# Three PSUM banks in turn for layer 2 and one for layer 1, in place of two and two

## The chip, the cores and the metric

The kernel runs on one core of a Trainium2 chip, alone. The metric is the device time of one execution in microseconds; the time of a kernel is the median of its runs.

## The reference

The input `x` has 2 x 4096 tokens of 192 numbers. Three things are done to it, and only the first looks at more than one token:

```python
out = np.einsum('hk,bskhg->bshg', softmax(weight), x_unf)   # causal, 7 taps, 8 heads of 24
h = x @ w_in;  g = h * np.clip(h + 3, 0, 6) / 6;  x = g @ w_out      # layer 1, 192 -> 2048 -> 192
h = x @ w_in
P = a[0] + a[1]*h + a[2]*h**2 + a[3]*h**3
Q = 1 + abs(b[0])*abs(h) + abs(b[1])*h**2
x = (P / (Q + 1e-6)) @ w_out                                          # layer 2, the same sizes
```

All of it is float32. The kernel makes each float32 product of sums of products of a high and a low part, so that one layer's tile takes several matmuls.

## The kernel before, in words

The 8192 tokens are cut into 16 blocks of 512; the last block is cut in two once more, so there are 17 units (0 to 14 whole, 15 and 16 of 256 tokens). The 2048 hidden numbers are cut into 16 parts of 128. One tile is 128 hidden numbers of a unit, 128 x 512 elements; a unit of half width takes two parts at once, so that its tiles have that shape as well. Each layer has 15 x 16 + 2 x 8 = 256 tiles, and the planner's time runs in steps of one tile of layer 2.

A tile of layer 1: five matmuls `mm1` (L501) put h into a PSUM bank; ACT makes `u` from it (L545), DVE makes `g` from `u` and the bank (L550), and with that the bank is free; ACT rounds the high part (`hi1`, L557), POOL takes the low part (`lo1`, L563), and five matmuls (`mm2` and `mm2l`, L515 to L520) add it to the unit's two sums in other banks. After 16 tiles the sums become the input of layer 2.

A tile of layer 2: five matmuls `mm3` (L501) put h into a bank; ACT makes `A` = |h| (L615) and `T` (`t1`, L627), DVE two steps of the numerator (`t2` L642, `t3` L654, both read the bank), ACT or POOL and then POOL make the denominator `S` (L634, L636, L648), ACT its reciprocal root (`R`, L659), whose square (`RR`, L663) is written into the bank, DVE a Newton step (`w` L668), the numerator's last step, into the bank (`p2` L672), and the product `G` (L677), and with that the bank is free. Then `hi2` on ACT (L683), `lo2` on POOL (L692), and five matmuls `mm4` and `mm4l`.

PSUM has eight banks. Four hold the sums of the two layers. The other four are `bank0` to `bank3` (L218): layer 1 takes 0 and 1 in turn (`site1`, L522; in the beginning unit 0 has bank 0 and unit 1 bank 1), layer 2 takes 2 and 3 in turn (`site2`, L528; in the last unit, two tiles in four take 0 and 1). A third kind of work needs a bank for a short time: the convolution (`conv`, L442, on xn), the transposes of its result (`flip`, L457) and of the output (`out_tr`, L708 and L709). `transient` (L769) gives them the bank that layer 1 does not use at that moment, `1 - [...]` of the list `line1`. While the weights are being split into high and low parts, in the first 19 steps, banks 2 and 3 also serve as scratch for that (`weights`, L727).

In SBUF, T, S, A, g2h and g2l of layer 2 have two buffers each (pool `p2`), u, g1h and g1l of layer 1 two each (`p1`). The weights come in through four buffers `raw` of 128 x 1024 (pool `sg`) and five `m` of 128 x 512 (`sgm`), which have little to do later.

The order on every engine is fixed ahead by the class `Issue`. Each operation is entered with `at` (L83) under an engine, a duration, what it reads and writes, and a sort key: its step plus an offset from `OFF` (`OFF0` in the beginning, `OFFT` in the last unit). `graph` (L87) derives the dependences, also those from a ring of buffers or a bank that comes round, and `order` (L125) lists the operations engine by engine: of those that are ready it takes the one with the smallest key plus a bias of its kind, within a look-ahead (`AHEAD`, `LOOK`). The engines run these lists strictly in order. Layer 1 runs ahead: its units 0 and 1 go together in steps 0 to 16 (`when1`, L756), then one unit per 17 steps; layer 2 begins in step 19 (`LAG`) with one unit per 16 steps (`when2`, L763). Layer 1 is done some 12 steps before layer 2.

Of the kernel before, what the change touches and what calls it, by code (L numbers as in the profile page):

```python
# [7 lines left out]
F32 = mybir.dt.float32  # L8
F32R = mybir.dt.float32r
# [5 lines left out]
D1 = 2  # L15
# [2 lines left out]
PER = 17  # L18
PERH = 13
CONV = -11  # L20
CONV2 = 1.4221
PAT = [1, 2]
PAT0 = [1, 2]
PATT = [1, 2]
W1P = [-2.7212, -2.1926]
W2P = [2.853, 2.0712]
WARM = 12
LOENG = [0, 1, 0, 1]
CLAMP = [0, 1, 0, 1]
WPART = dict(c0=0.0035, v0=-0.1744, vs=0.2224, h0=0.4972, hs=0.0194, l0=0.7095, ls=0.0191)  # L30
HEAD = 19.51
TAIL = -8.47
AHEAD0 = dict(P=23.739, A=33.318, V=6.679, G=43.933, S=999.0)
LOOK0 = dict(P=22, A=218, V=3, G=275, S=0)
AHEADT = dict(P=10.587, A=26.994, V=26.868, G=6.693, S=999.0)
LOOKT = dict(P=716, A=250, V=265, G=983, S=0)
OFF0 = dict(
    mm2=-1.6078, mm2l=-1.3327, x2mh=-0.6482, x2mg=-0.8371, lo1=1.3047, x2ml=-0.5563, x2al=-1.1236, x2mc=-0.2459,
    mm1=-0.2559, hi1=0.8615, g=0.1758, u=0.1648, x2ah=-1.1817,
)  # L40
OFFT = dict(
    sq=0.2665, mm4l=-0.2221, x2al=3.1822, RR=1.6307, q2=1.4163, oa=-0.1248, lo2=4.0164, mm3=-0.5662, q1=1.0926,
    A=-0.4555, t3=0.9018, w=2.2795, G=3.1778, x2mh=1.9241, x2mg=2.1784, x2ml=2.9393, hi2=3.9844, R=1.562,
    p2=2.2993, tr=0.9036, q=1.6358, os=1.3787, mm4=-0.289, x2mc=3.187,
)
D10 = 3
D2T = 5
X0 = -5.1761
X1 = -0.8706
XW = [-103.8655, -103.0862, -56.7048, -45.6279]  # L50
BIAS = dict(l1=1.269, dec=1.5585, conv=1.482, out=-3.4178, x2=0.5443)
AHEAD = dict(P=10.034, A=30.747, V=25.077, G=8.984, S=999.0)
LOOK = dict(P=11, A=158, V=144, G=308, S=0)
OFF = dict(
    sq=-0.1906, q1=-0.0053, q2=0.0282, mm3=-0.5496, mm1=1.0929, mm4=0.0716, tr=1.357, mm2=1.3942, A=-0.5102,
    t1=0.082, u=1.2441, R=0.2631, RR=0.3824, hi2=1.3091, hi1=2.1384, S=-0.339, lo2=1.8031, lo1=2.9099,
    q=-3.3161, t2=0.2092, t3=0.3818, w=0.5827, p2=0.9559, G=1.047, g=1.2615, cv=1.6807, x1ah=1.6042,
    x1al=1.9194, x1bh=1.5836, x1bl=1.795, x2ah=2.2232, x2al=3.1818, x2mh=1.7614, x2mg=2.9447, x2mc=2.2852,
    x2ml=1.8296, oa=0.8152, oc=0.9804, os=1.5101, mm2l=1.6382, mm4l=0.4334,
)  # L60


class Issue:
# [10 lines left out]
        mm1=1133, mm3=1133, conv=774, flip=445, out_tr=533, u=477, hi1=520, hi2=520, t1=568, R=520, RR=520,  # L74
# [106 lines left out]
def conv_moe_moe_kernel(ctx: ExitStack, tc: tile.TileContext, x, weight, w_in1, w_out1, w_in2, w_out2,  # L181
# [8 lines left out]
    B, S, DM = x.shape  # L190
# [5 lines left out]
    C = 512  # L196
# [4 lines left out]
    NU = len(units)  # L201
    steps = [NF * n // C for _, _, n in units]
# [4 lines left out]
    p1 = ctx.enter_context(tc.tile_pool(name="p1", bufs=2))  # L207
    p2 = ctx.enter_context(tc.tile_pool(name="p2", bufs=2))
# [4 lines left out]
    sgm = ctx.enter_context(tc.tile_pool(name="sgm", bufs=5))  # L213
# [4 lines left out]
    bank = [ps.tile([128, C], F32, name=f"bank{k}") for k in range(4)]  # L218
# [95 lines left out]
    raw = {}  # L314
# [207 lines left out]
    def site1(b, i):  # L522

        if b == 1:
            return p2, ("T", "g2h", "g2l"), 1
        return p1, ("u", "g1h", "g1l"), i % 2 if b else 0

    def site2(b, i):  # L528

        if b == NU - 1 and i % 4 >= 2:  # L530
            return p1, ("raw", "raw", "m", "g1h", "g1l"), i % 2
        return p2, ("S", "T", "A", "g2h", "g2l"), 2 + i % 2

    class L1:
        @staticmethod
# [57 lines left out]
    class L2:  # L593
# [5 lines left out]

        @staticmethod  # L600
        def mm3(b, i):
            h2[b, i] = bank[site2(b, i)[2]]
            product_in(1, b, i, [x2[b, k] for k in ("x2ah", "x2al", "x2m1", "x2ml")], h2[b, i])

        @staticmethod
        def A(b, i):
            v2[b, i] = d = {}
            p, tags, _ = site2(b, i)
            if tags[0] == "raw":
                st = sg.tile([128, 2 * C], F32, tag="raw", name="ST")  # L610
# [12 lines left out]

        @staticmethod
# [102 lines left out]
    def weights(t_load, t, kind, l, c, turn):  # L727
# [40 lines left out]

    def transient(t, mm, ns, *args, r, kind):  # L769

        if t > end1 or mm in (conv, flip) and args[0] == 1:
            k = fill[0] = fill[0] + 1
            tag = f"acc{int(t < end1)}{k % 2}"
            key = (tag, ("free", k))
            at(t, "P", ns, mm, lambda: pa.tile([128, C], F32, tag=tag, name="fb"), *args, r=r, w=[key], kind=kind)
        else:
            k = fill[0] % 2 if t < 0 else 0 if t < steps[0] else 1 - [k for w, k in line1 if w <= t][-1]
            fill[0] += 1
            key = (f"bank{k}", ("free", fill[0]))
            at(t, "P", ns, mm, lambda: bank[k], *args, r=r, w=[key], kind=kind)  # L780
        return key

    fill = [0]
    taken = {when1(b, 0) + CONV + k for b in range(2, NB) for k in range(4)}
    for b in range(NU):
        bl, _, cols_u = units[b]
        for i in range(steps[b]):
            n, t, c = (b, i), when1(b, i), i * C // cols_u // 2
            _, (U, Hi, Lo), k = site1(b, i)
            U, Hi, Lo, k = (U, (1, n)), (Hi, (1, n)), (Lo, (1, n)), (f"bank{k}", (1, n))  # L790
# [14 lines left out]
            _, (S_, T, A, Hi, Lo), k = site2(b, i)
            if S_ == "raw":
                S_, T = ("raw", n), ("rawT", n)
            else:
                S_, T = (S_, n), (T, (2, n))
            A, Hi, Lo, k = (A, n), (Hi, (2, n)), (Lo, (2, n)), (f"bank{k}", (2, n))  # L810
# [36 lines left out]
        t = when2(b, steps[b] - 1) + (D2T if b == NU - 1 else D2)  # L847
# [3 lines left out]
        for hf in range(cols_u // 256):  # L851
            t = int(t + 1.9)
# [10 lines left out]
        t = when1(b, 0) + CONV if not first else X1 if b else X0  # L863
# [98 lines left out]
```

## Time and profile before

| | us |
|---|---|
| median of 3 runs | 1310.19 (1309.35 to 1311.1) |
| the profiled execution | 1310.59 |
| its span, first to last instruction | 1308.8 |

The span is 1.79 us shorter than the time of the same execution. Busy time of an engine is the time in which at least one of its instructions runs; matmuls overlap, and their ends are modelled, so that PE counts as busy also where the next matmul starts a little late. PEld is the weight load that precedes each matmul. Idle time of an engine that isn't the bottleneck costs nothing.

### The profile page before, as it was taken

The page shows a single profiled execution, that of the slowest core. Times are in us where ns is not written, and L with a number is a line of the kernel's source. Part 1 is how long each engine was busy: PE and PEld are TensorE (multiplying, and loading weights), DVE is VectorE, ACT ScalarE, POOL GpSimd, SP SyncE. Part 2 cuts the span into 40 slices and gives each one's busy share as a digit, 9 for nine tenths or more (in the row PEclk, how much of TensorE's full clock was granted, in tenths as well). Part 3 has the DMA queues.
Part 4 walks back from the last instruction along what each step waited for, and adds up shares of the span by engine and source line. Part 5 has one row for each costly group of instructions (what it writes and reads, how often), then busy time and mean ns, then how long its engine had stood idle before and what let it go on. Part 6 is the DMA issues. An engine that isn't in the chain of part 4 may idle for free.

```text
span 1308.8 us, 18723 instructions
## 1 busy us (share of the span) xinstructions
PE 1277.1 (98%) x6072; PEld 1039.8 (79%) x6072; DVE 1164.5 (89%) x1808; ACT 1192.1 (91%) x2183; POOL 1123.6 (86%) x954
## 2 busy tenths in 40 slices
PE   8999999999999999999999999999999999999977
PEld 5776877878788888888888888888787888888866
DVE  6999898988988889889898898988989889898897
ACT  5788999999999999999999999999999999999996
POOL 4998898888898888988889888888988898888976
PEclk9999999999999999999999999999999999999998
DMA  6440000000000000000000000000000000000000
GB/s 176 139 151 18 16 1 13 16 7 22 1 14 14 13 16 7 22 1 13 16 13 16 13 1 17 13 16 13 1 28 0 2 13 1 13 2 13 1 13 13
DMA packets 29002, 28.62 MB, mean 22 GB/s; under 512 B 2156, under 2 KB 25832, under 8 KB 28904
## 3 DMA queue, kind: packets, MB, share of 16 engines
q1 hardware_dynamic: 28744, 27.27, 7.0%
q8 instruction: 47, 0.77, 0.2%
q14 instruction: 51, 0.42, 0.1%
q10 hardware_dynamic: 160, 0.16, 0.0%
HBM read 21.13 MB, written 6.30 MB: 21 GB/s over the span
## 4 chain that ended last, share of the span: by engine, by line
PE 64%; DVE 16%; ACT 15%; issue 3%; POOL 2%; DMA 1%; SPq 0%; DVEq 0%; ACTq 0%; POOLq 0%
PE bank L501 30%; PE acc L518 6%; PE acc L515 6%; PE acc L520 6%; PE acc L519 6%; PE acc L516 6%; ACT bank L663 2%; DVE bank L672 2%; DVE S L668 2%; DVE T L654 2%; DVE T L677 2%; ACT A L659 2%; PE bank L442 2%; DVE T L642 2%; ACT A L615 2%
## 5 line engine op out<-in xcount | busy, mean ns | idle before, releaser
L648 POOL TENSOR_TENSOR S<-A,S 128x512 f32<-128x512 f32 x252 | 327.0, 1298 | 73.9 <-ACT S L634 56.2
L692 POOL TENSOR_TENSOR g2l<-T,g2h 128x512 fp32r<-128x512 f32 x252 | 327.7, 1301 | 47.7 <-ACT g2h L683 45.0
L563 POOL TENSOR_TENSOR g1l<-u,g1h 128x512 fp32r<-128x512 f32 x240 | 311.8, 1300 | 6.5 <-ACT g1h L557 4.6
L668 DVE SCALAR_TENSOR_TENSOR S<-S,bank 128x512 f32<-128x512 f32 x252 | 172.6, 685 | 80.6 <-ACT bank L663 75.1
L501 PE MATMUL bank<-low,B 128*128 128x512 f32 (+1 forms) x544 | 205.4, 378 | 0.0
L654 DVE SCALAR_TENSOR_TENSOR T<-T,coef,bank 128x512 f32<-128x512 f32 x252 | 188.3, 747 | 8.3
L672 DVE SCALAR_TENSOR_TENSOR bank<-T,coef,bank 128x512 f32<-128x512 f32 x252 | 188.9, 749 | 0.4
L642 DVE SCALAR_TENSOR_TENSOR T<-T,coef,bank 128x512 f32<-128x512 f32 x252 | 186.8, 741 | 2.0 <-ACT T L627 1.7
L550 DVE SCALAR_TENSOR_TENSOR u<-u,bank 128x512 f32<-128x512 f32 x240 | 163.1, 681 | 18.6 <-ACT u L545 18.1
L677 DVE SCALAR_TENSOR_TENSOR T<-S,bank 128x512 f32<-128x512 f32 x252 | 172.8, 686 | 7.2
L683 ACT ACTIVATE g2h<-T 128x512 fp32r<-128x512 f32 x252 | 159.3, 632 | 20.9 <-DVE T L677 17.8
L663 ACT ACTIVATE bank<-A 128x512 f32<-128x512 f32 x256 | 153.2, 598 | 24.4 <-DVE T L654 20.2
L627 ACT ACTIVATE T<-bank,coef 128x512 f32<-128x512 f32 x252 | 173.5, 688 | 1.8 <-POOL g2l L692 1.7
L659 ACT ACTIVATE A<-S 128x512 f32<-128x512 f32 x252 | 157.8, 626 | 13.2 <-POOL S L648 12.2
L557 ACT ACTIVATE g1h<-u 128x512 fp32r<-128x512 f32 x240 | 151.4, 632 | 10.2 <-DVE u L550 9.9
L545 ACT ACTIVATE u<-bank 128x512 f32<-128x512 f32 x240 | 141.6, 592 | 4.2 <-PE bank L501 2.9
L501 PE MATMUL bank<-x2ah,Ah 128*128 128x512 f32 (+1 forms) x272 | 110.3, 406 | 12.5 <-DVE T L677 9.9
L636 POOL TENSOR_SCALAR S<-A,coef 128x512 f32<-128x512 f32 x126 | 98.1, 779 | 24.1 <-ACT A L615 23.1
L501 PEld LDWEIGHTS bank<-low,B 128*128 128x128 f32 x544 | 102.4, 188 | 19.6
L515 PE MATMUL acc<-g2l,O 128*128 128x512 f32 (+1 forms) x280 | 111.5, 400 | 1.7 <-POOL g2l L692 1.4
L518 PE MATMUL acc<-g2h,O 128*128 128x512 f32 (+1 forms) x280 | 108.4, 387 | 1.5 <-ACT g2h L557 0.7
L501 PE MATMUL bank<-x1ah,Ah 128*128 128x512 f32 (+1 forms) x272 | 105.1, 386 | 3.2 <-DVE u L550 2.9
(135 smaller groups left out, 3216.6 us busy)
## 6 DMA issues: line engine op xcount, KB each, us to landing
raw<-in_moe_w_out_dram SPq DMA_DIRECT2D x16, 384.0 KB, 3.7
out_dram<-osb SPq DMA_DIRECT2D x32, 192.0 KB, 2.0
xn<-in_x_dram SPq DMA_DIRECT2D x14, 384.0 KB, 3.4
raw<-in_moe_w_in_dram SPq DMA_DIRECT2D x16, 256.0 KB, 2.9
raw<-in_moe_w_in_dram SPq DMA_DIRECT2D x16, 128.0 KB, 3.4
xn<-in_x_dram SPq DMA_DIRECT2D x16, 96.0 KB, 3.2
xn<-in_x_dram SPq DMA_DIRECT2D x2, 288.0 KB, 6.3
band<-line_d SPq DMA_DIRECT2D x2, 256.0 KB, 3.9
```

What stands on the lines that cost most here:

```text
L501: nc.tensor.matmul(out=dst[:, cs], lhsT=w[nm][:, fs], rhs=m, start=(k == 0), stop=(k == 4))
L515: nc.tensor.matmul(out=a, lhsT=o[:, 0:128], rhs=g, start=False, stop=sp)
L518: nc.tensor.matmul(out=a, lhsT=o[:, 0:128], rhs=g, start=st, stop=False)
L563: nc.gpsimd.tensor_tensor(out=gl, in0=v1.pop((b, i)), in1=f32(g1[b, i][0]), op=ALU.subtract)
L642: stt(out=d["T"], in0=d["T"], scalar=coef[:, 2:3], in1=h2[b, i], op0=ALU.add, op1=ALU.mult)
L648: (nc.gpsimd if k else nc.vector).tensor_tensor(out=d["S"], in0=d["A"], in1=d["S"], op=ALU.add if k == 1 else ALU.mult)
L654: stt(out=d["T"], in0=d["T"], scalar=coef[:, 1:2], in1=h2[b, i], op0=ALU.add, op1=ALU.mult)
L659: act(out=d["A"], in_=d["S"], func=ACTF.Abs_reciprocal_sqrt, bias=c1)
L668: stt(out=d["S"], in0=d["S"], scalar=c1, in1=h2[b, i], op0=ALU.add, op1=ALU.mult)
L672: stt(out=h2[b, i], in0=v2[b, i]["T"], scalar=coef[:, 0:1], in1=h2[b, i], op0=ALU.add, op1=ALU.mult)
L677: stt(out=d["T"], in0=d["S"], scalar=2.0, in1=h2.pop((b, i)), op0=ALU.subtract, op1=ALU.mult)
L692: e.tensor_tensor(out=gl, in0=v2.pop((b, i))["T"], in1=f32(gh), op=ALU.subtract)
```

## The change

Layer 1 has only bank 0 (and unit 1, as before, bank 1). Layer 2 takes banks 3, 1, 2 in turn, and in the last unit every fourth tile takes bank 0. The buffers go with the bank: tiles on banks 2 and 3 use the pool `p2` as before, a tile on bank 1 has S and T in a `raw` buffer and A, g2h and g2l in `m` buffers, a tile on bank 0 has S and T in two `u`, A in an `m`, and `g1h` and `g1l`. So T, for one, has three places in place of two. A transient takes the bank of the next tile of layer 2 that begins more than 1.2 steps after it (`NEXT`). All sort keys and most biases and look-aheads get other values; the operations, their engines, forms and number stay the same, and so do `LAG`, `PER`, `PERH`, D1 and D2.

```diff
-        return p1, ("u", "g1h", "g1l"), i % 2 if b else 0
+        return p1, ("u", "g1h", "g1l"), 0
+
+    def spare2(b, i):
+        return b == NU - 1 and i % 4 == 3
+
+    turn2 = {}
+    for u in range(NU):
+        for i in range(steps[u]):
+            turn2[u, i] = 0 if spare2(u, i) else 1 + (2 + sum(v > 0 for v in turn2.values())) % 3
 
     def site2(b, i):
-        if b == NU - 1 and i % 4 >= 2:
-            return p1, ("raw", "raw", "m", "g1h", "g1l"), i % 2
-        return p2, ("S", "T", "A", "g2h", "g2l"), 2 + i % 2
+        k = turn2[b, i]
+        return (("u", "u", "m", "g1h", "g1l"), ("raw", "raw", "m", "m", "m"))[k] if k < 2 else ("S", "T", "A", "g2h", "g2l"), k
+
+    def place2(b, i, j):
+        tag = site2(b, i)[0][j]
+        p = dict(u=p1, g1h=p1, g1l=p1, m=sgm).get(tag, p2)
+        t = p.tile([128, C], F32R if tag[0] == "g" else F32, tag=tag, name=tag)
+        return t.bitcast(F32R) if tag == "m" and j > 2 else t
...
-    line1 = [(when1(u, i), i % 2) for u in range(NU) if u != 1 for i in range(steps[u])]
+    line2 = [(when2(u, i), turn2[u, i]) for u in range(NU) for i in range(steps[u])]
...
-            k = fill[0] % 2 if t < 0 else 0 if t < steps[0] else 1 - [k for w, k in line1 if w <= t][-1]
+            k = fill[0] % 2 if t < 0 else 0 if t < steps[0] else [k for w, k in line2 if w + NEXT > t][0]
```

Of the keys in `OFF`, those that the prediction speaks of (in steps; before, after): mm1 1.0929, 0.3745; u 1.2441, 0.6259; g 1.2615, 0.8453; mm3 -0.5496, -0.4599; t1 0.082, 0.1215; G 1.047, 1.3429; lo2 1.8031, 2.5013; tr (a transient's matmuls) 1.357, 1.7345; cv (the convolution's copy out) 1.6807, 2.4719.

## Rows read from the trace of the kernel before

**Rows 1.** the page's first part: busy us (share of the span) xinstructions of each engine

```profile
PE 1277.1 (98%) x6072; PEld 1039.8 (79%) x6072; DVE 1164.5 (89%) x1808; ACT 1192.1 (91%) x2183; POOL 1123.6 (86%) x954
```

**Rows 2.** stretches: from:to us, length, engine busy us (xcount), PE clock, DMA share, GB/s

```profile
20.60:112.70 92.10, 85.60 (x375) 64.70 (x373) 86.44 (x176) 73.89 (x156) 79.75 (x76) 1.00 0.44 131
112.70:1244.00 1131.30, 1125.36 (x5311) 921.40 (x5311) 1012.31 (x1516) 1061.28 (x1926) 993.92 (x827) 1.00 0.04 11
1244.00:1300.80 56.80, 44.86 (x303) 40.41 (x304) 52.82 (x81) 48.15 (x87) 43.64 (x38) 0.93 0.04 11
1300.80:1308.80 8.00, 3.81 (x23) 3.45 (x22) 1.12 (x2) 1.51 (x3) 0.01 (x1) 0.71 0.08 26
```

**Rows 3.** the same view, a stretch of eight whole units of layer 2

```profile
410.80:1013.60 602.80, 602.43 (x2770) 491.19 (x2769) 539.51 (x807) 567.02 (x1028) 530.05 (x441) 1.00 0.04 12
```

**Rows 4.** groups by line on PE in that stretch; xcount, busy us, mean ns, idle before

```profile
L442 PE MATMUL bank<-xn,band 128*122 128x120 f32 x112 | 14.4, 272 | 0.1
L709 PE MATMUL bank<-perm,oac 128*128 128x64 f32 x64 | 9.9, 248 | 0.0
L457 PE MATMUL bank<-perm,x1n 122*128 122x122 f32 (+1 forms) x70 | 9.6, 267 | 0.0
```

**Rows 5.** that stretch, line 677 alone (once per tile of layer 2)

```profile
410.80:1013.60 602.80, 87.77 (x128) 1.00 0.04 12
```

**Rows 6.** that stretch, line 550 alone (once per tile of layer 1)

```profile
410.80:1013.60 602.80, 81.58 (x120) 1.00 0.04 12
```

**Rows 7.** timeline, PE: start us, duration us, engine, line, operation [idle before <-releaser]

```profile
700.75 0.39 PE L501 MATMUL bank<-x1ah,Ah 128*128 128x512 f32 x1
...
701.88 0.39 PE L501 MATMUL bank<-x2ah,Ah 128*128 128x512 f32 x1
...
706.55 0.39 PE L501 MATMUL bank<-x2ah,Ah 128*128 128x512 f32 x1
...
707.69 0.39 PE L501 MATMUL bank<-x1ah,Ah 128*128 128x512 f32 x1
...
710.41 1.01 PE L442 MATMUL bank<-xn,band 128*122 128x120 f32 x8
...
711.18 0.48 PE L501 MATMUL bank<-x2ah,Ah 128*128 128x512 f32 x1
```

**Rows 8.** timeline, ACT and DVE, the same stretch

```profile
708.38 0.59 ACT L545 ACTIVATE u<-bank 128x512 f32<-128x512 f32 x1
...
709.12 0.68 DVE L550 SCALAR_TENSOR_TENSOR u<-u,bank 128x512 f32<-128x512 f32 x1
...
709.43 0.61 ACT L545 ACTIVATE u<-bank 128x512 f32<-128x512 f32 x1
...
709.72 0.68 DVE L677 SCALAR_TENSOR_TENSOR T<-S,bank 128x512 f32<-128x512 f32 x1
...
711.46 0.57 ACT L450 ACTIVATE x1n<-bank 122x480 f32<-122x480 f32 x1 [0.38 <-PE bank L442]
...
711.76 0.68 DVE L550 SCALAR_TENSOR_TENSOR u<-u,bank 128x512 f32<-128x512 f32 x1
```

**Rows 9.** waits from 130 to 1177 us: who waited for whom: us, times, longest us

```profile
DVE S L668 <- ACT bank L663: 67.7, 138, 1.4
...
PEld bank L501 <- DVE T L677: 15.7, 51, 1.0
...
PEld bank L442 <- DVE u L550: 2.5, 8, 0.6
...
PEld bank L708 <- DVE u L550: 1.7, 5, 0.5
...
PEld bank L501 <- DVE u L550: 1.3, 3, 0.6
```

**Rows 10.** waits from 1225 us to the end

```profile
PEld bank L501 <- DVE T L677: 10.0, 9, 2.1
```

More of the change, by code (lines that the diff above doesn't have):

```diff
@@ L20 @@
 CONV = -11
-CONV2 = 1.4221
+CONV2 = 1.5208
 PAT = [1, 2]
@@ L24 @@
 PATT = [1, 2]
-W1P = [-2.7212, -2.1926]
-W2P = [2.853, 2.0712]
+W1P = [-2.511, -1.6167]
+W2P = [3.1007, 2.6842]
 WARM = 12
@@ L29 @@
 CLAMP = [0, 1, 0, 1]
-WPART = dict(c0=0.0035, v0=-0.1744, vs=0.2224, h0=0.4972, hs=0.0194, l0=0.7095, ls=0.0191)
+WPART = dict(c0=0.0894, v0=0.1498, vs=0.1355, h0=1.0583, hs=0.051, l0=1.1051, ls=0.1176)
 HEAD = 19.51
 TAIL = -8.47
[L33 to L36, printed above, removed]
+AHEAD0 = dict(P=29.159, A=34.598, V=14.704, G=33.913, S=999.0)
@@ L37 @@
+LOOK0 = dict(P=181, A=111, V=0, G=135, S=0)
+AHEADT = dict(P=2.417, A=11.5, V=26.627, G=8.091, S=999.0)
+LOOKT = dict(P=52, A=118, V=110, G=1311, S=0)
 OFF0 = dict(
-    mm2=-1.6078, mm2l=-1.3327, x2mh=-0.6482, x2mg=-0.8371, lo1=1.3047, x2ml=-0.5563, x2al=-1.1236, x2mc=-0.2459,
-    mm1=-0.2559, hi1=0.8615, g=0.1758, u=0.1648, x2ah=-1.1817,
+    mm2=-1.5338, mm2l=-1.3337, x2mh=-0.4568, x2mg=0.4102, lo1=1.1872, x2ml=-0.3679, x2al=0.2982, x2mc=0.2088,
+    mm1=-1.0623, hi1=0.8438, g=-0.5149, u=-0.6917, x2ah=-0.9173,
@@ L40 @@
 )
 OFFT = dict(
-    sq=0.2665, mm4l=-0.2221, x2al=3.1822, RR=1.6307, q2=1.4163, oa=-0.1248, lo2=4.0164, mm3=-0.5662, q1=1.0926,
-    A=-0.4555, t3=0.9018, w=2.2795, G=3.1778, x2mh=1.9241, x2mg=2.1784, x2ml=2.9393, hi2=3.9844, R=1.562,
-    p2=2.2993, tr=0.9036, q=1.6358, os=1.3787, mm4=-0.289, x2mc=3.187,
+    sq=-0.3575, mm4l=-1.2305, x2al=3.5317, RR=2.1537, q2=1.3964, oa=-1.0444, lo2=3.4316, mm3=-0.3947, q1=1.2682,
+    A=-0.3856, t3=1.0523, w=2.4254, G=2.4661, x2mh=1.7969, x2mg=2.2183, x2ml=2.2136, hi2=3.3057, R=2.0466,
@@ L45 @@
+    p2=2.4646, tr=1.3163, q=1.0405, os=5.7408, mm4=-1.4005, x2mc=3.3094,
 )
 D10 = 3
+NEXT = -1.2
 D2T = 5
[L48 to L53, printed above, removed]
-OFF = dict(
[L55 to L59, printed above, removed]
+X0 = -4.2712
@@ new lines @@
+X1 = -0.9752
+XW = [-101.8602, -99.0414, -56.2823, -44.9956]
+BIAS = dict(l1=0.2014, dec=0.3628, conv=0.3916, out=-6.738, x2=-1.6469)
+AHEAD = dict(P=26.611, A=26.201, V=45.444, G=12.098, S=999.0)
+LOOK = dict(P=4, A=153, V=220, G=328, S=0)
+OFF = dict(
+    sq=0.078, q1=0.159, q2=0.352, mm3=-0.4599, mm1=0.3745, mm4=0.9141, tr=1.7345, mm2=1.5094, A=-0.395,
+    t1=0.1215, u=0.6259, R=0.698, RR=0.8701, hi2=2.3581, hi1=1.7962, S=0.2827, lo2=2.5013, lo1=2.5753,
+    q=-0.6239, t2=0.2901, t3=0.693, w=1.0533, p2=1.185, G=1.3429, g=0.8453, cv=2.4719, x1ah=2.174, x1al=2.1763,
+    x1bh=1.8025, x1bl=2.4464, x2ah=1.749, x2al=2.9755, x2mh=2.1412, x2mg=3.1559, x2mc=2.984, x2ml=2.795,
+    oa=1.0447, oc=1.0665, os=1.8428, mm2l=1.6702, mm4l=0.9897,
@@ L601, in mm3 @@
         def mm3(b, i):
-            h2[b, i] = bank[site2(b, i)[2]]
+            h2[b, i] = bank[site2(b, i)[1]]
             product_in(1, b, i, [x2[b, k] for k in ("x2ah", "x2al", "x2m1", "x2ml")], h2[b, i])
@@ L606, in A @@
         def A(b, i):
-            v2[b, i] = d = {}
-            p, tags, _ = site2(b, i)
-            if tags[0] == "raw":
+            d = v2.setdefault((b, i), {})
+            if site2(b, i)[0][0] == "raw":
                 st = sg.tile([128, 2 * C], F32, tag="raw", name="ST")
                 d["S"], d["T"] = st[:, 0:C], st[:, C:2 * C]
-                d["A"] = sgm.tile([128, C], F32, tag="m", name="A")
-            else:
-                d["A"] = p.tile([128, C], F32, tag="A", name="A")
+            d["A"] = place2(b, i, 2)
             act(out=d["A"], in_=h2[b, i], func=ACTF.Abs, scale=coef[:, 4:5] if form(b, i) == 1 else 1.0)
@@ L618, in tile @@
         def tile(b, i, k):
-            d = v2[b, i]
+            d = v2.setdefault((b, i), {})
             if k not in d:
-                d[k] = p2.tile([128, C], F32, tag=k, name=k)
+                d[k] = place2(b, i, "ST".index(k))
             return d[k]
@@ L680, in hi2 @@
         def hi2(b, i):
-            p, tags, _ = site2(b, i)
-            g2[b, i] = [p.tile([128, C], F32R, tag=tags[3], name=tags[3])]
+            g2[b, i] = [place2(b, i, 3)]
             act(out=g2[b, i][0], in_=v2[b, i]["T"], func=ACTF.Copy)
@@ L686, in lo2 @@
         def lo2(b, i):
-            p, tags, _ = site2(b, i)
-            gl = p.tile([128, C], F32R, tag=tags[4], name=tags[4])
+            gl = place2(b, i, 4)
             gh = g2[b, i][0]
@@ L764, in when2 @@
         return start2[u] + i
-    line1 = [(when1(u, i), i % 2) for u in range(NU) if u != 1 for i in range(steps[u])]
-    end1 = line1[-1][0] + D1 + 1.99
+    line2 = [(when2(u, i), turn2[u, i]) for u in range(NU) for i in range(steps[u])]
+    end1 = when1(NU - 1, steps[-1] - 1) + D1 + 1.99
     def transient(t, mm, ns, *args, r, kind):
@@ L804, in conv_moe_moe_kernel @@
             f = form(b, i)
[L805 to L810, printed above, removed]
+            (S_, T, A, Hi, Lo), k = site2(b, i)
+            S_, T = (S_, ("S", n)), ("rawT" if T == "raw" else T, (2, n))
+            A, Hi, Lo, k = (A, ("A", n)), (Hi, (2, n)), (Lo, (3, n)), (f"bank{k}", (2, n))
             ac = [(f"acc1{j}", (1, b)) for j in range(2)]
```

## The prediction

> **What bounds the kernel now.** I read the page's busy times first [rows 1]: PE counts as busy for 98% of the span, ACT for 91%, DVE for 89%, POOL for 86%. PE's share says little by itself, since a matmul is listed with 0.39 us while the next begins sooner, so that a matmul that starts 0.1 us late leaves no idle time. So I counted PE's work by starts. From one first matmul to the next over five lie 1.13 us (700.75 to 701.88) and 1.14 us (706.55 to 707.69) [rows 7]: 0.227 us each.
>
> Then the stretches [rows 2]. From 20.6 to 112.7 us only layer 1 runs, with the splitting of the weights beside it, and DVE is busy for 86.44 of 92.1 us: DVE is the bound there. From 112.7 to 1244 us both layers run. From 1244 to 1300.8 us layer 2 is alone, and DVE is again the bound, 52.82 of 56.8 us. The last 8 us are the drain behind the last tile.
>
> For the long middle I took a stretch of eight whole units of layer 2, 602.8 us [rows 3]. It holds 128 tiles of layer 2 and 120 of layer 1 [rows 5, 6], so one tile of layer 2 every 4.71 us and one of layer 1 every 5.02 us. PE begins 2770 matmuls in it; 112 belong to the convolution, 70 to its transposes, 64 to the output's, with 32 wider ones that go with those [rows 4], 278 in all. The other 2492 at 0.227 us are 565.7 us. Eight of the convolution take 0.77 us up to the next start (710.41 to 711.18 [rows 7]), 0.096 each, and at that price the 278 are 26.7 us. Sum 592.4 us: PE is late by only 10.4 of 602.8 us, 1.7%. ACT, with 567.02 us or 94%, comes next [rows 3]. So **PE's matmuls bound the middle**, and over its 1131.3 us the whole that can be won there is 1131.3 x 10.4 / 602.8 = 19.5 us. This change takes no matmul away.
>
> What makes PE late stands in the waits from 130 to 1177 us [rows 9]. The largest, 15.7 us in 51 times, is mm3 waiting for `G` (L677) to free a bank of layer 2. The waits on `g` of layer 1 (L550) are 2.5 us of the convolution, 1.7 us of the output's transposes and 1.3 us of mm1 itself: 5.5 us. The four make 21.2 us by the weight loads; a load waits a little before the matmul would be late, so that this agrees with the 19.5.
>
> One tile shows why mm3 waits. It takes its bank at 701.88, and `G` ends at 709.72 + 0.68 = 710.40: held for 8.5 us. The second mm3 behind it, on the same bank, starts at 711.18, 9.30 us after the first [rows 7, 8]. So the two banks of layer 2 are full for 8.5 of 9.3 us.
>
> **The change, part by part.**
>
> *Third bank for layer 2.* A tile may now hold its bank for three tiles, 3 x 4.71 = 14.1 us, in place of 9.4. If the hold stayed at 8.5 us, 5.6 us would be free between two tiles. The new keys use some of it: from mm3 to G they go from 1.60 to 1.80 steps, about 0.9 us more, and the tile T, from t1 to lo2, from 1.72 to 2.38 steps, for which the third set of buffers is there. Price of the stall: at most the 15.7 us [rows 9], at least nothing gained, if the next engine in line is as late. Next is ACT: at 94% and in order, it is what DVE already waits for at L668 for 67.7 us [rows 9]. With 10 us less over the middle ACT would stand at 95%, so there is still room. I take two thirds of it, **-10 us**, nearer to the whole than to nothing, since a wait that 5 us of slack cover ends for a tile that was 0.3 us late on average (15.7 / 51).
>
> *One bank for layer 1.* Today a tile is let to wait: the mm1 of 700.75 has its u at 708.38 and its g ends at 709.80, 9.05 us held; that of 707.69 has u at 709.43 and g until 712.44, 4.75 us [rows 7, 8]. With one bank, every hold must stay under the 5.02 us of a tile. The least that it can be: mm1 1.14 us to the last start and 0.16 us more to its listed end, u 0.59, g 0.68, together 2.6 us and the hand-overs between three engines. The new keys ask for that: u 0.25 and g 0.47 steps after mm1 (1.2 and 2.2 us; before 0.15 and 0.17 steps, which the engines didn't follow). So some 2 us of slack are left, if ACT and DVE bring u and g forward. Bounds: the 1.3 us of today go, or mm1 becomes what PE waits for (the second rival). I take **+1 us**.
>
> The Trainium skill has a rule against this part: "Perfetto Trace Analysis", section "Matmuls", says that independent groups of matmuls should rotate through different PSUM banks, so that the evacuation of one overlaps with the next. By the rule alone layer 1 loses that overlap in every tile. The rows above speak against a loss here, since between two mm1 PE has the other matmuls of both layers to run.
>
> *Transients go to layer 2's banks.* The 44 of the stretch (14 convolutions, 14 transposes, 16 of the output) lose the wait on g, 4.2 us, and get a wait on G; the convolution of 710.41 holds its bank until its copy ends at 712.03, 1.6 us [rows 7, 8], which fits the 4.7 us left by then. But the keys set its copy only 0.74 steps behind it, nearly at the mm3 for which the bank is meant. Bounds -4.2 and +4.2 us; I take 0.
>
> *The beginning.* Bank use is the same there; only keys move. DVE could win its idle time, 92.1 - 86.44 = 5.7 us [rows 2], or lose as much: 0.
>
> *The end.* mm3 waits 10.0 us for G in the last 84 us [rows 10], but DVE is the bound, and in the last stretch only 56.8 - 52.82 = 4.0 us of it are idle. Three banks instead of two help the unit before the last (the last one had four already): between 0 and -4, I take **-2 us**. In the drain nothing changes.
>
> *Buffers.* The operations move to other SBUF tiles in the same shapes; they're priced at nothing, since the splitting of weights that shares raw and m is over before the second tile of layer 2.
>
> Sum: -10 + 1 + 0 + 0 - 2 = -11 us. The profiled execution took 1310.59 us, so 1299.6; it lies 0.40 above the median, so by the median 1299.2: **1299 us**. A measurement of this kernel can tell 0.2%, 2.6 us, from no change.
>
> **The rivals.**
>
> *PE gets dense.* With both layers' hand-overs loosened, all that PE is late in the middle goes, 19.5 us, and 2 us at the end and 2 us in the beginning: 1310.2 - 23.5, about 1287 us. For it: the waits on banks are nearly all that PE is late for. Against it: ACT at 94% would be the next to be late. Chance 0.15.
>
> *The wait moves on.* The bank is free earlier, but mm3 or the matmuls behind it wait as long for g2 or for ACT's order, or the transients eat the third bank, so that the change doesn't give layer 2 what it says: 1308 to 1311 us. For it: the 67.7 us that DVE waits for ACT today. Against it: PE, not DVE, is the bound of the middle. Chance 0.12.
>
> *Layer 1's single bank stalls PE: slower.* Its place is mm1, behind the u on ACT and the g on DVE of the tile before. One late bank costs PE some 0.4 us (1.3 us in 3 waits [rows 9]), and whatever stands behind mm1 in PE's list waits too. The middle has 1131.3 / 5.02 = 225 tiles of layer 1; if one in four is late, that is 56 x 0.43 = 24 us, less the 12 won elsewhere: 1310 + 12 = 1322 us. It decides from 12 / 0.43 = 28 late tiles on, one in eight. For it: today's holds of 9.05 and 4.75 us, 6.9 on average, are above 5.02. Against it: the 2.4 us by which the least hold stays below it. This is also where the skill's rule on rotating banks would lead. Chance 0.19.
>
> **How the numbers follow.** The forecast, 1293 to 1306 us, has 0.54; with the dense PE that makes 0.69 for faster, 0.12 for within 0.2%, 0.19 for slower. The range goes from 1286, half of the dense case, to 1316, a good third of the way that the slower case covers; below lie some 0.07, above some 0.12.
>
> **What would show it.** Right: mm3's waits on G fall from 15.7 to under 6 us between 130 and 1177 us, PE starts its 2770 matmuls of eight units in some 597 us, and u follows mm1 in under 2.5 us. Wrong: new waits of mm1 on g above 10 us, waits of the convolution on G, eight units that still take 602 us, or a beginning or an end that is 3 us longer than its row.

## The result and the profile after

The changed kernel takes 1288.01 us in the median of 4 runs (1286.76 to 1288.92), the one before 1310.48 beside it: ratio 0.9829, 95% interval 0.9812 to 0.9846, or 22.5 us less. The span of the profiled execution went from 1308.8 to 1285.5 us, 23.3 us less.

The page's first part, after [rows 1]:

```profile
PE 1264.5 (98%) x6072; PEld 1042.9 (81%) x6072; DVE 1139.2 (89%) x1808; ACT 1182.8 (92%) x2183; POOL 1119.7 (87%) x954
```

The engines' shares are what they were. The view of stretches shows more, cut where layer 2 begins, where its last whole unit (14) begins and where its last unit (16) begins. Ahead of it, the kernel before cut at the same places; its first stretch is that of [rows 2]:

```profile
112.70:1164.30 1051.60, 1048.48 (x4835) 853.79 (x4836) 940.90 (x1409) 988.16 (x1793) 922.95 (x768) 1.00 0.04 11
1164.30:1262.90 98.60, 92.19 (x590) 81.35 (x588) 87.99 (x134) 90.11 (x165) 84.57 (x72) 1.00 0.03 9
1262.90:1308.80 45.90, 33.35 (x212) 30.12 (x212) 37.35 (x57) 32.67 (x58) 30.06 (x26) 0.86 0.03 9
```

After:

```profile
19.70:105.70 86.00, 83.57 (x369) 64.06 (x368) 81.59 (x167) 70.76 (x150) 77.52 (x75) 1.00 0.46 140
105.70:1149.20 1043.50, 1039.25 (x4832) 857.22 (x4830) 922.03 (x1414) 982.86 (x1797) 920.78 (x770) 1.00 0.04 11
1149.20:1244.50 95.30, 93.43 (x606) 83.78 (x605) 90.44 (x143) 91.72 (x170) 86.78 (x73) 1.00 0.03 9
1244.50:1285.50 41.00, 31.39 (x208) 28.28 (x206) 33.21 (x52) 30.29 (x56) 28.39 (x25) 0.91 0.03 11
```

With nearly the same number of matmuls in each (369 against 375, 4832 against 4835, 814 against 802 in the last two), the gain falls in three parts: layer 2 begins at 105.7 in place of 112.7 us, **7.0 us**; the middle up to unit 14 takes 1043.5 in place of 1051.6, **8.1 us**; the rest 136.3 in place of 144.5, **8.2 us**. TensorE's granted clock reads 1.00 in every stretch up to unit 16 in both kernels, and in the last one, where DVE is the busiest engine, 0.86 and 0.91; so the clock is no part of what was won up to there.

The eight units of the middle [rows 3]:

```profile
403.80:999.70 595.90, 595.51 (x2759) 491.78 (x2758) 527.29 (x806) 561.28 (x1027) 527.79 (x441) 1.00 0.04 12
```

595.9 in place of 602.8 us. By the prediction's prices, 2759 - 278 matmuls at 0.227 and 26.7 us for the 278 are 589.9: PE is late by 6.0 us there, before by 10.4. So 4.4 of the 6.9 us are PE's lateness. The other 2.5 are the price of the 11 matmuls that the stretch now holds less, about one tile of layer 1, which are done elsewhere and so not saved; over the 1051.6 us up to unit 14, 4.4 in 602.8 us make some 7.7, which agrees with the 8.1.

The waits from 130 to 1160 us (those of [rows 9] go up to 1177; L680, L565 and L689 are what L668, L550 and L677 were; ST is a `raw` buffer, which holds S and T of a tile on bank 1):

```profile
DVE S L680 <- ACT bank L675: 33.6, 51, 1.6
...
DVE ST L680 <- ACT bank L675: 19.6, 30, 1.7
...
PEld bank L502 <- DVE T L689: 3.4, 7, 0.7
...
PEld bank L502 <- DVE u L565: 2.9, 13, 0.3
...
PEld bank L502 <- DVE ST L689: 1.6, 4, 0.6
```

The weight loads' waits on G are 3.4 + 1.6 = 5.0 us in place of 15.7, those of mm1 on g 2.9 in place of 1.3.

How the banks are held shows in the timeline, first PE, then DVE:

```profile
664.43 0.39 PE L502 MATMUL bank<-x2ah,Ah 128*128 128x512 f32 x1
...
665.56 0.39 PE L502 MATMUL bank<-x1ah,Ah 128*128 128x512 f32 x1
...
669.92 0.47 PE L502 MATMUL bank<-x1ah,Ah 128*128 128x512 f32 x1
...
677.34 0.39 PE L502 MATMUL bank<-x2ah,Ah 128*128 128x512 f32 x1
```

```profile
669.16 0.68 DVE L565 SCALAR_TENSOR_TENSOR u<-u,bank 128x512 f32<-128x512 f32 x1
...
675.87 0.68 DVE L689 SCALAR_TENSOR_TENSOR T<-S,bank 128x512 f32<-128x512 f32 x1
```

The tile of 664.43 frees its bank at 675.87 + 0.68 = 676.55 us, after 12.1 us, and its bank's next tile comes at 677.34; in [rows 7, 8] it was 8.5 of 9.3 us. Layer 1's tile of 665.56 holds bank 0 until 669.84, 4.3 us in place of 4.75 and 9.05, and the next mm1 starts at 669.92. Over all tiles of the eight units, matched in their order, layer 2's hold is 10.9 us on average, before 9.0, and layer 1's 3.4 us, before 6.0; the tile with 9.05 us in the prediction was the longest of them. From the end of g to the next mm1 on bank 0 lie 1.6 us on average, but in 15 of 120 tiles less than 0.5, as in the tile shown. So layer 2's hold has grown with its banks, and layer 1's has shrunk into its one. The u starts 1.8 us after mm1 on average (3.7 before), in 100 of 120 tiles under 2.5.

### The profile page after: what moved, and what is told of

Read it like the earlier page. It is cut to its first block, busy times and chain, and to the rows that moved or that the text cites. A ratio compares the mean times of both kernels' runs of the same rounds, so it can differ in the third digit from the quotient of the medians.

```text
span 1285.5 us, 18778 instructions
## 1 busy us (share of the span) xinstructions
PE 1264.5 (98%) x6072; PEld 1042.9 (81%) x6072; DVE 1139.2 (89%) x1808; ACT 1182.8 (92%) x2183; POOL 1119.7 (87%) x954
## 4 chain that ended last, share of the span: by engine, by line
PE 81%; DVE 8%; ACT 7%; issue 2%; POOL 1%; DMA 1%; SPq 0%; DVEq 0%; POOLq 0%; ACTq 0%
PE bank L502 39%; PE acc L516 8%; PE acc L519 8%; PE acc L517 8%; PE acc L520 7%; PE acc L521 7%; PE bank L443 2%; PE bank L458 1%; DVE bank L371 1%; PE bank L719 1%; ACT bank L675 1%; DVE bank L684 1%; DVE bank L368 1%; PE bank L718 1%; DVE T L565 1%
## 5 line engine op out<-in xcount | busy, mean ns | idle before, releaser
L702 POOL TENSOR_TENSOR g2l<-T,g2h 128x512 fp32r<-128x512 f32 x169 | 219.6, 1300 | 23.2 <-ACT g2h L694 19.3
L660 POOL TENSOR_TENSOR S<-A,S 128x512 f32<-128x512 f32 x169 | 219.5, 1299 | 19.7 <-ACT S L646 12.0
L565 DVE SCALAR_TENSOR_TENSOR u<-u,bank 128x512 f32<-128x512 f32 x240 | 164.0, 683 | 38.9 <-ACT u L560 32.2
L572 ACT ACTIVATE g1h<-u 128x512 fp32r<-128x512 f32 x240 | 151.1, 629 | 1.6 <-PE acc L521 0.6
L680 DVE SCALAR_TENSOR_TENSOR S<-S,bank 128x512 f32<-128x512 f32 x169 | 115.6, 684 | 38.9 <-ACT bank L675 35.7
L654 DVE SCALAR_TENSOR_TENSOR T<-T,coef,bank 128x512 f32<-128x512 f32 x169 | 125.6, 743 | 12.3 <-ACT T L639 11.2
L684 DVE SCALAR_TENSOR_TENSOR bank<-T,coef,bank 128x512 f32<-128x512 f32 x169 | 126.7, 750 | 0.1
L666 DVE SCALAR_TENSOR_TENSOR T<-T,coef,bank 128x512 f32<-128x512 f32 x169 | 125.5, 743 | 0.8
L702 POOL TENSOR_TENSOR m<-ST,m 128x512 fp32r<-128x512 f32 x85 | 110.6, 1301 | 12.6 <-ACT m L694 11.6
L660 POOL TENSOR_TENSOR ST<-m,ST 128x512 f32<-128x512 f32 x85 | 110.3, 1298 | 10.7 <-ACT ST L646 4.7
L689 DVE SCALAR_TENSOR_TENSOR T<-S,bank 128x512 f32<-128x512 f32 x169 | 115.5, 683 | 2.6
L639 ACT ACTIVATE T<-bank,coef 128x512 f32<-128x512 f32 x169 | 116.3, 688 | 1.1 <-POOL g2l L702 0.9
L694 ACT ACTIVATE g2h<-T 128x512 fp32r<-128x512 f32 x169 | 106.6, 631 | 4.3 <-DVE T L689 3.6
L502 PE MATMUL bank<-x1ah,Al 128*128 128x512 f32 (+1 forms) x272 | 103.1, 379 | 0.8 <-DVE Al L396 0.8
```

Of the source, the lines that this page charges most:

```text
L502: nc.tensor.matmul(out=dst[:, cs], lhsT=w[nm][:, fs], rhs=m, start=(k == 0), stop=(k == 4))
L565: stt(out=t, in0=t, scalar=1.0, in1=h1.pop((b, i)), op0=ALU.min, op1=ALU.mult)
L572: act(out=gh, in_=v1[b, i], func=ACTF.Copy)
L639: act(out=v2[b, i]["T"], in_=h2[b, i], func=ACTF.Copy, scale=coef[:, 3:4])
L654: stt(out=d["T"], in0=d["T"], scalar=coef[:, 2:3], in1=h2[b, i], op0=ALU.add, op1=ALU.mult)
L660: (nc.gpsimd if k else nc.vector).tensor_tensor(out=d["S"], in0=d["A"], in1=d["S"], op=ALU.add if k == 1 else ALU.mult)
```

## The experiments

Each ratio is against the kernel before on the same chip, with its 95% interval.

**The constants of the beginning, taken back.** Everything else as changed:

```diff
-W1P = [-2.511, -1.6167]
+W1P = [-2.7212, -2.1926]
...
-AHEAD0 = dict(P=29.159, A=34.598, V=14.704, G=33.913, S=999.0)
+AHEAD0 = dict(P=23.739, A=33.318, V=6.679, G=43.933, S=999.0)
```

(with CONV2, W2P, WPART, LOOK0, OFF0, X0, X1 and XW in the same way)

> The changed kernel with the constants of the beginning as they were before (keys of OFF0, the weights' keys, the look-ahead of the first 19 steps); banks, buffers and all later keys stay changed. The first mm3 came at 112.7 us before and 105.7 us after. Theory 1 (7 us of the gain are a better order of the beginning and have nothing to do with banks): first mm3 near 112 us, the whole near 1295 us. Rival (the beginning is faster since layer 1's third unit has another bank): first mm3 stays near 106, the whole near 1288.

Measured 1289.98 us, 0.9846 (0.983 to 0.9863). The first mm3 in the timeline:

```profile
112.33 0.39 PE L502 MATMUL bank<-x2ah,Ah 128*128 128x512 f32 x1
```

It is back at 112.33, 6.6 us later, but the span is only 3.1 us longer (1288.6) and the median 2.0: half or more of a later start is made up before the end. Theory 1 has the place right and the worth wrong.

**The same constants alone in the kernel before.**

> The kernel before with only the constants of the beginning of the changed one. Theory 1: first mm3 near 106 us in place of 112.7, and since all that follows is as before, 1310.5 - 7 = 1303.5 us. Rival (the new order of the beginning needs the new banks): 1310 us or more.

Measured 1310.21 us, 1.0008 (0.9999 to 1.0018); the first mm3 came at 113.6 us. Without the rest they're worth nothing. So the 7 us at the beginning explain little of the whole, some 2 to 3 of the 22.5 us.

**The new banks with the old keys.**

```diff
-OFF = dict(sq=0.078, q1=0.159, q2=0.352, mm3=-0.4599, mm1=0.3745, ...
+OFF = dict(sq=-0.1906, q1=-0.0053, q2=0.0282, mm3=-0.5496, mm1=1.0929, ...
```

(and all other keys, biases and look-aheads)

> The banks and buffers of the change with every key, bias and look-ahead of before. Theory 2 (the third bank itself takes the wait off, whatever the keys): the wait of mm3 on G falls from 15.7 us to under 6, eight units of layer 2 in some 596 us, the whole near 1295 us (beginning as before). Rival (the keys of before let layer 1 hold its bank for 5 to 9 us, and with one bank mm1 becomes what PE waits for): waits of mm1 on g of over 20 us, the whole above 1315 us.

Measured 1319.23 us, 1.007 (1.0055 to 1.0085): slower than before. Eight units in the view of stretches, and the waits:

```profile
414.50:1016.50 602.00, 598.59 (x2754) 488.89 (x2754) 536.87 (x804) 561.14 (x1025) 526.55 (x440) 1.00 0.04 12
```

```profile
PEld bank L502 <- DVE T L689: 6.6, 8, 1.4
...
PEld bank L502 <- DVE u L565: 4.3, 16, 0.6
...
PEld bank L502 <- DVE ST L689: 3.0, 4, 1.2
```

602.0 us, as before, with 9.6 us of weight loads waiting on G and 4.3 on g: neither theory's number. By the prediction's prices PE is late by 13.2 us there, more than the 10.4 of before. The last mm1 came at 1255.9 us, 25 later than before, and with it the end. Banks and buffers without their keys bring nothing; the order must be made for them.

**The new keys with the old banks.** Three sets of buffers stay:

```diff
-        return p1, ("u", "g1h", "g1l"), 0
+        return p1, ("u", "g1h", "g1l"), i % 2 if b else 0
...
-        ... if k < 2 else ("S", "T", "A", "g2h", "g2l"), k
+        ... if k < 2 else ("S", "T", "A", "g2h", "g2l"), i % 2 if b == NU - 1 and i % 4 >= 2 else 2 + i % 2
...
-    ... [k for w, k in line2 if w + NEXT > t][0]
+    ... 1 - [k for w, k in line1 if w <= t][-1]
```

> The changed kernel with two banks for each layer as before (transients on layer 1's other bank), but with the three sets of buffers and all keys of the change, except that the convolution's copy and one low part come 0.17 and 0.15 steps earlier, so that a transient leaves layer 1's bank in time. Theory 3 (keys and third bank bring the gain only together: the keys hold a bank for 9 us and more, which needs three): mm3's waits on G of over 40 us between 130 and 1160 us, the whole slower than before, above 1325 us. Rival (the keys with the third set of buffers bring it, the banks don't matter): 1290 to 1296 us.

Measured 1352.15 us, 1.0323 (1.0308 to 1.0339). The three longest waits of PE's weight loads (L572 is hi1, which writes g1h, and L519 a matmul of mm2):

```profile
PEld bank L502 <- DVE T L689: 10.5, 25, 2.3
...
PEld acc L519 <- ACT g1h L572: 8.9, 11, 1.7
...
PEld bank L502 <- DVE ST L689: 5.1, 10, 1.4
```

As slow as theory 3 said and more, but the loads' waits on G are 15.6 us, not over 40; a two-bank layout in this order makes PE wait for layer 1's g1h as well. These waits don't add up to the 42 us. From 420 to 1045 us PE's mean granted clock is also 0.99 in place of 1.00; the rest of the cause stays open.

**Two sets of buffers, and its control.** Both have hi2 at 1.95 and lo2 at 2.05 steps; the first also has

```diff
-        ... ("raw", "raw", "m", "m", "m"))[k] if k < 2 else ("S", "T", "A", "g2h", "g2l"), k
+        ... ("raw", "raw", "m", "m", "m"))[k] if k < (2 if b == NU - 1 else 1) else ("S", "T", "A", "g2h", "g2l"), k
```

> The changed kernel with two sets of S, T, A, g2h, g2l for three banks (three sets only in the last unit), and the keys of hi2 and lo2 set to 1.95 and 2.05 steps, so that T lives less than two tiles. Theory 4 (the third set of buffers is as needed as the third bank, since T is held from t1 to lo2, 8.6 us on average before): above 1305 us, with waits of t1 on g2l (L702). Rival (the bank alone brings it): within 4 us of the next run.

> The control for the run before: the changed kernel, three sets of buffers, with the same two keys (hi2 1.95, lo2 2.05). Expected within 5 us of the changed kernel, 1288 to 1293 us, by all theories.

Two sets: 1323.87 us, 1.0106 (1.0089 to 1.0123); three: 1293.38, 0.9874 (0.9859 to 0.9888). The two-set run's profiled execution was its longest, 1328.87 us. The waits, first with two sets, then with three (L702 is lo2, L694 hi2, L654 t2 and L639 t1; with three sets a tile on bank 1 has `m` and ST in place of g2l and T):

```profile
POOL g2l L702 <- ACT g2h L694: 48.0, 61, 3.4
...
DVE T L654 <- ACT T L639: 26.8, 58, 1.7
...
ACT T L639 <- POOL g2l L702: 2.0, 6, 0.5
```

```profile
POOL g2l L702 <- ACT g2h L694: 33.8, 55, 2.9
...
POOL m L702 <- ACT m L694: 20.2, 22, 3.2
...
DVE T L654 <- ACT T L639: 8.1, 16, 1.6
...
DVE ST L654 <- ACT ST L639: 5.2, 12, 1.3
```

With these keys the third set is worth 30 us. But the wait of t1 on lo2 that was expected is 2.0 us. POOL's wait on hi2 is 48.0 us with two sets and 33.8 + 20.2 = 54.0 with three, so it isn't that either; DVE's wait on t1 is 26.8 in place of 8.1 + 5.2 = 13.3. Where the 30 us go isn't shown, and keys borrowed from another layout are no fair test of one. So three layouts got keys of their own.

**One part alone, with its own keys.** The first is the layout of the two-set run, the second that of the two-bank run, the third is the kernel before.

> Three banks for layer 2 and one for layer 1, with two sets of buffers (three only in the last unit), and keys searched anew for this layout, by the durations that the planner itself carries. Theory 5 (third bank and third set are needed together: T must be given back within two tiles, so the bank's slack can't be used): 1303 to 1313 us, near the kernel before. Rival (the 1323.87 us of the run with borrowed keys came from the keys; the bank alone is enough): 1293 us or less.

> Two banks for each layer, with three sets of buffers, and keys searched anew for this layout in the same number of trials. Theory 5: the third set is of no use where the bank must come back within two tiles, 1305 to 1315 us, mm3's waits on G near the 15.7 us of before. Rival (the third set of buffers or the search is what brought the gain): 1296 us or less.

> The kernel before, banks and buffers unchanged, with keys searched anew in the same number of trials: what a search alone is worth. Theory 5 (the keys of before suit their layout already): 1306 to 1312 us. Rival (the gain of the change is a better search): 1296 us or less.

Measured: third bank alone 1302.02 us, 0.9942 (0.9927 to 0.9957); third set alone 1300.58, 0.9933 (0.9918 to 0.9948); neither 1306.28, 0.9976 (0.9966 to 0.9985). So a search is worth 3.2 us in the old layout, and either part alone 4 to 6 us more (the first two also have the changed kernel's constants of the beginning, the third has those of before): theory 5 is missed by 1 us by the first and by 4 us by the second (its loads wait for G 4.3 us, not 15.7), and holds for the third. The eight units of each, in that order:

```profile
405.70:1001.40 595.70, 594.99 (x2755) 490.08 (x2754) 538.20 (x802) 561.70 (x1023) 526.27 (x438) 1.00 0.04 12
```

```profile
407.10:1004.10 597.00, 596.86 (x2767) 493.60 (x2766) 540.30 (x807) 568.14 (x1028) 527.80 (x441) 1.00 0.04 13
```

```profile
408.70:1010.00 601.30, 600.57 (x2766) 491.51 (x2765) 541.01 (x808) 567.06 (x1029) 529.53 (x442) 1.00 0.04 12
```

595.7, 597.0 and 601.3 us; by the prediction's prices PE is late by 6.7, 5.3 and 9.8 us: in the middle **either part alone does what both do** (595.9, late by 6.0). Theory 5 falls there. The loss of the two lies at the beginning (first mm3 at 111.2 and 111.8 us) and at the end. In the first one mm1 does wait for its single bank, 9.8 us in 35 times, with PE late by only 0.7 us more in the eight units. One thing these runs leave open: the changed kernel's keys weren't made by this search, so how much of the 13 to 14 us between them is the layout and how much the keys isn't shown.

**Layer 1 keyed later.**

```diff
-    ... u=0.6259 ... g=0.8453
+    ... u=1.0759 ... g=1.2953
```

> The changed kernel with u and g of layer 1 keyed 0.45 steps (2.1 us) later, so that each tile holds bank 0 longer; nothing else changes. Theory 6 (with its own keys layer 1 leaves bank 0 some 2 us before the next mm1, and that margin is what makes one bank free of charge): the waits of mm1 on g rise from 2.9 us to over 15 us and the whole to 1297 us or more. Rival (one bank has slack enough anyway): waits under 6 us, 1288 to 1291 us.

Measured 1296.79 us, 0.9904 (0.9889 to 0.9918). The waits:

```profile
DVE S L680 <- ACT bank L675: 53.3, 61, 2.1
DVE ST L680 <- ACT bank L675: 33.5, 40, 1.4
...
PEld bank L502 <- DVE u L565: 3.0, 11, 0.5
```

The time comes within 0.2 us of theory 6's least, the cause isn't its own: mm1 waits no longer than before for g. The hold of bank 0 grew only from 3.4 to 4.25 us on average, and from g to the next mm1 0.8 us are left in place of 1.6; half the margin is gone and the waits are the same. What grew is DVE's wait on ACT's square of the root, from 33.6 + 19.6 to 86.8 us. That u and g, keyed later, stand in the way of layer 2's chain would explain it, but wasn't tested.

**The end: two banks in unit 14 alone.** While layer 1 does its last, half-wide units, 8 tiles in 13 steps, layer 2 could go faster. The timeline of PE shows the first and last mm3 of unit 14, the last mm1 and the first mm3 of unit 16; the kernel before, then the changed one:

```profile
1164.31 0.40 PE L501 MATMUL bank<-x2ah,Ah 128*128 128x512 f32 x1
...
1231.14 0.28 PE L501 MATMUL bank<-x1ah,Ah 128*128 128x256 f32 x1
...
1232.22 0.40 PE L501 MATMUL bank<-x2ah,Ah 128*128 128x512 f32 x1
...
1262.92 0.38 PE L501 MATMUL bank<-x2ah,Ah 128*128 128x256 f32 x1 [1.75 <-DVE T L677]
```

```profile
1149.20 0.40 PE L502 MATMUL bank<-x2ah,Ah 128*128 128x512 f32 x1
...
1210.23 0.39 PE L502 MATMUL bank<-x2ah,Ah 128*128 128x512 f32 x1
...
1227.37 0.28 PE L502 MATMUL bank<-x1ah,Ah 128*128 128x256 f32 x1
...
1244.53 0.33 PE L502 MATMUL bank<-x2ah,Ah 128*128 128x256 f32 x1
```

From the first mm3 to that of the sixteenth tile it takes 67.9 us, 4.53 a tile, before; 61.0, 4.07 a tile, after. When the last mm1 starts, 239 tiles of layer 2 are begun before and 244 after; unit 16 then begins 31.8 and 17.2 us later. The run with a third set but two banks goes as the kernel before, 66.6 us or 4.44 a tile:

```profile
1153.91 0.40 PE L492 MATMUL bank<-x2ah,Ah 128*128 128x512 f32 x1
...
1220.51 0.40 PE L492 MATMUL bank<-x2ah,Ah 128*128 128x512 f32 x1
```

The other runs agree: the old layout with keys searched anew, two banks, takes 4.51 us a tile; the new banks with the keys of before, three banks, take 4.06.

But a faster layer 2 is no time won in this stretch. The view of stretches from the first mm3 of unit 14 to the last mm1, before and after:

```profile
1164.30:1231.10 66.80, 65.39 (x409) 58.32 (x408) 60.22 (x92) 61.77 (x113) 59.54 (x51) 1.00 0.02 7
```

```profile
1149.20:1227.30 78.10, 77.61 (x479) 68.58 (x478) 73.88 (x116) 75.19 (x139) 71.65 (x60) 1.00 0.02 6
```

PE is full in both. By starts (0.227 us for each of 150 and 180 whole matmuls, 0.12 for each of 245 and 285 half-wide ones, some 1 us for the other 12; an estimate) it is late by only 2 us in either. So the five tiles, 5 x 10 x 0.227 = 11.3 us of PE, and the 3.8 us by which the last mm1 comes earlier are no more than the 15.1 us won ahead of unit 14. What the five tiles save comes behind the last mm1: there a tile takes 3.4 us (17 tiles in 57.9 us up to the last mm3 before, 12 in 41.2 after), with DVE the busiest engine, so five cost 16.7 us in place of PE's 11.3. These 5.4 us, and 2.9 us less behind the start of the last mm3, make up the 8.2 us of the end (to within 0.1). Why the 2.9 came is open.

To see what the bank does there, one run takes the third bank away here and nowhere else:

```diff
+    def bank2(b, i):
+        return 3 - i % 2 if b == NU - 3 else turn2[b, i]
...
-        ... ("S", "T", "A", "g2h", "g2l"), k
+        ... ("S", "T", "A", "g2h", "g2l"), bank2(b, i)
...
-    line2 = [(when2(u, i), turn2[u, i]) for u in range(NU) for i in range(steps[u])]
+    line2 = [(when2(u, i), 1 if u == NU - 3 else turn2[u, i]) for u in range(NU) for i in range(steps[u])]
```

> The changed kernel with two banks (3 and 2 in turn) for the 16 tiles of unit 14 alone, the last whole unit, in which layer 1 thins out; its transients go to bank 1, which is idle there; buffers and keys stay. Theory 7 (in this unit, not in the middle, the bank count sets layer 2's pace: a hold of some 9 us on two banks allows a tile every 4.5 us, on three banks DVE and ACT allow one every 4.1, and each tile that layer 2 is behind when layer 1 ends costs DVE's 3.6 us at the end): unit 14 takes 70 to 73 us in place of 65.0, 239 to 241 tiles of layer 2 are begun at the last mm1 in place of 244, and the whole is 1296 to 1300 us. Rival (the end is set by when layer 1 ends): unit 14 slower, but the whole at 1288 to 1291 us.

Measured 1299.27 us, 0.9919 (0.9904 to 0.9934): 11.3 us of the gain are gone. Timeline and waits from 1150 to 1240 us:

```profile
1151.77 0.39 PE L502 MATMUL bank<-x2ah,Ah 128*128 128x512 f32 x1
...
1222.16 0.45 PE L502 MATMUL bank<-x2ah,Ah 128*128 128x512 f32 x1
...
1231.38 0.28 PE L502 MATMUL bank<-x1ah,Ah 128*128 128x256 f32 x1
...
1256.23 0.28 PE L502 MATMUL bank<-x2ah,Ah 128*128 128x256 f32 x1
```

```profile
PEld bank L502 <- DVE T L692: 5.1, 6, 2.6
```

From the first mm3 of unit 14 to its last are 70.4 us, 4.69 a tile (61.0 after; the 65.0 of the theory counts one tile more, and by that measure it would be some 75); 242 tiles are begun at the last mm1 (two of them of unit 15, let ahead by the idle bank), and unit 16 begins 24.85 us behind it. The time is theory 7's and not the rival's; the tiles are one more than it said. The last mm1 itself came 4.0 us later (1231.38), so not all of the 11.3 is backlog: two tiles at 3.4 us are 6.8.

This isn't how the kernel before lost its time. From the first mm3 of unit 14 to the last mm1:

```profile
1151.80:1231.30 79.50, 73.65 (x426) 64.08 (x425) 67.00 (x102) 67.54 (x123) 64.29 (x54) 0.96 0.02 6
```

By the same starts PE is late by 11 us here, and its mean granted clock is 0.96, lowest (0.69 over 4 us) in and behind its two longest pauses, at 1188 and 1224 us; in the kernel before PE was late by 2, and in unit 14 its loads waited for G once, 1.6 us. With the changed kernel's keys the third bank in unit 14 is worth 11.3 us. What it would be worth with keys made for two banks in that unit wasn't run.

**Two sets up to unit 13, three behind.**

```diff
-        ... [k] if k < 2 else ...
+        ... [k] if k < (2 if b >= NU - 3 else 1) else ...
```

(with keys of its own)

> Three banks and one; two sets of buffers in units 0 to 13, three only in the last three units; keys searched anew for this layout. Theory 8 (through the middle the third bank alone is enough, and the 14 us that the two-set run with its own keys stayed behind were lost in the beginning and in the last units): eight units in 595 to 598 us, 243 or more tiles of layer 2 begun at the last mm1, the whole 1288 to 1295 us. Rival (the third set is needed all along): 1300 us or more.

Measured 1296.23 us, 0.9894 (0.9877 to 0.991), 1.2 us above what theory 8 said. Its eight units:

```profile
406.00:1002.60 596.60, 596.08 (x2755) 490.13 (x2754) 538.47 (x803) 562.55 (x1024) 526.71 (x439) 1.00 0.04 12
```

596.6 us, PE late by 7.6, and 246 tiles begun at the last mm1: the third bank is enough in the middle. The 8 us to the changed kernel go with a first mm3 at 111.65 us, 5.9 later than there, and a last mm1 at 1240.6, 13 us later. With 0.6 us between g and the next mm1, mm1 waits 10.7 us for g.

## Why the prediction was right, and where it was not

The sign was right and 1288 us lies inside the range, 1286 to 1316, but near its edge: of the 11 us forecast it became 22.5, outside the likely band of 1293 to 1306. The value is that of the rival in which PE gets dense, but its reason is not: PE is still late by 6.0 of the 10.4 us in eight units. Two of the three signs came: mm3's waits on G are 5.0 us, and the eight units take 595.9. The third, u under 2.5 us behind mm1, came in 100 of 120 tiles.

- *Third bank for layer 2, -10 us.* About the right size: 8.1 us up to unit 14, and 4.4 of the 10.4 us of lateness in eight units. The mechanism, mm3's wait on G, went from 15.7 to 5.0 us. But the price was given to the bank alone. The runs show that the third set of buffers alone does as much there, and that the two together do nothing in the old order (1319.23 us). Layer 2's hold grew by some 2 us, twice the 0.9 of the prediction.
- *One bank for layer 1, +1 us.* Right: 1.3 us of waits became 2.9. The holds shrank from 6.0 to 3.4 us on average, as the new keys asked. The 6.9 us that the second rival took for today's average came from two tiles, one of them the longest. The margin of some 2 us came out as 1.6. The rule of the Trainium skill on rotating banks ("Perfetto Trace Analysis", section "Matmuls"), which spoke against this part, would have cost every tile its overlap; this trace shows 1.6 us more of waits, with other matmuls between two mm1.
- *Transients, 0.* The waits of the convolution and of the output's transposes on g, 4.2 us, are gone; in their place stand 0.7 + 0.5 = 1.2 us of the output's transposes on G, and none of the convolution.
- *The beginning, 0.* Wrong in size: layer 2 starts 7.0 us earlier. The run with the old constants shows that half or more of it is made up later anyway, 3.1 us being left in the span and 2.0 in the median. The constants alone don't bring it: with them the first mm3 comes at 113.6 us with the old banks and keys, at 112.0 with the old banks and the new keys, and at 111.2 with the new banks and other keys. Why stays open.
- *The end, between 0 and -4, taken as -2 us.* **This is the step that failed:** the end gave 8.2 us. I priced it from DVE's idle time in its last stretch, and so took the work that is left when layer 1 ends as fixed. It is not: 17 tiles of layer 2 were left then, and now 12. The time won ahead of unit 14, 15.1 us, let layer 2 do five tiles more beside layer 1, where a tile costs PE 2.27 us, in place of behind it, where it takes 3.4. That two banks, each held for 8.3 us a tile on average in unit 14 of the kernel before, keep layer 2 from going faster than some 4.5 us a tile fits all runs: with two banks 4.44 to 4.69, with three 4.01 to 4.21, or 4.37 with the two sets and borrowed keys. As a wait of the kernel before it doesn't show, so this much is argued.
- *The rival on the slower side* didn't come in this kernel. New banks with the old keys are 0.7% slower, with mm1's list 25 us late at the end, but mm1 waits only 4.3 us for g there, so its mechanism isn't shown. The two runs with 0.5 and 0.6 us between g and the next mm1 have 9.8 and 10.7 us of such waits, and are still faster than before.

So it was partly luck that the time fell inside the range: the middle was forecast well, but the beginning and the end, 15 us in the trace, were taken as 2. None of the twelve runs beats the changed kernel.

## What to carry to other kernels

Where two stages share an engine, ask how much of the one is left when the other ends, and which engine bounds that rest: time won earlier lets it shrink, and is then worth more than it was where it was won (15.1 us became 23.3 in the span here). A layout of banks and the fixed order of the instructions belong together: the one without the other was slower than neither (1319 and 1352 against 1310 us), so a layout is judged only with an order made for it. And one bank was enough for a stage that held it for 3.4 us of the 5.0 between its tiles; with holds of 4.4 and 4.5 us its waits were 10 us (130 to 1160 us).
